# Attention's first query tile in eight units of one batch instead of four of two, and a searched instruction order

## Chip, cores and metric

The kernel runs on one core of one Trainium2 chip. The metric is device microseconds of one execution (lower is better). The median of three executions before the change is 641.2 us (641.05 to 641.68); one further execution was profiled.

## Reference

Sliding-window attention with a linear distance bias, then a mixture of four experts with given probabilities, then one dense block with a squared ReLU:

```python
# q, k, v: [2 batches, 8 heads, 576 positions, 64]; window 128
scores = (q @ k.T) / sqrt(D) - slope[h] * |i - j|     # only 0 <= i - j < 128
attn   = exp(scores - max); attn = attn / (attn.sum(-1) + 1e-9)
x      = attn @ v                                     # reshaped to [1152 tokens, 512]
p      = domain_probs / (domain_probs.sum(-1) + 1e-9)
x      = sum_e p[:, e:e+1] * (relu(x @ w1[e]) @ w2[e])   # 4 experts, 512 -> 1024 -> 512
out    = (relu(x @ w_in) ** 2) @ w_out                # 512 -> 2048 -> 512
```

All inputs and the output are float32.

## The kernel before

**Stages.** Tokens are cut into four chunks (256, 256, 256 and 384 tokens). Attention works in units of query tiles: the first 128 queries of a batch (query tile 0, chunk 0) need only the first 128 keys. Later units cover two query tiles. Expert 0's first three chunks are interleaved with attention, so that TensorE (PE) has expert work to do while VectorE (DVE), ScalarE (ACT) and GpSimd (POOL) prepare the softmax. After that the kernel is a long row of expert matmuls, paced by another mechanism that the change does not touch.

**A unit of query tile 0** ("raw": plain float32, no split into a rounded part and a rest) runs these tasks: `sc` (L863 to L879: scores on PE), `mx` (`top`, L917: bias and running minimum, DVE), `ex` (L926: exp, ACT), `in` (L933, L937: sum and reciprocal, DVE), `no` (L942: normalise, DVE or POOL), `tp` (L966: transpose on PE), `hi` (copy the transposed tile to `pt`, ACT or DVE), `pv` (L764: times v, PE), `evx` (copy the result into the float32 tile `xfirst`), and later `evh` and `evl` (rounded part and rest, `xh` and `xl`). There are four such units; unit `c` holds heads `2c` and `2c+1` of both batches, that is four head squares of 128x128.

**First expert items.** Item `f` of chunk 0 computes 128 of the 1024 hidden columns: `g1.f` (first matmul), `hh` (ReLU), `g2.f` (second matmul into two `y` banks). Items 0 to 3 use `xfirst` and the weights as loaded, in float32, so they wait for no split: `g1` is four matmuls of 256 columns (L1839), one for each 128 rows of `xfirst` (so one for each unit), `g2` is L1790. Weight tiles of 512 KB are loaded in the order w1 part 0 (items 0 and 1), w2 part 0, w1 part 1 (items 2 and 3), w2 part 1, and so on. Items from 4 on use weights split by `weight_parts` (`wh`, `wl`) and run at L1051 and L1287.

**What sets the order.** A list planner (`Plan`) runs while the program is built. Each task has engine options with a modelled time (occupancy and latency), dependencies, buffer slots and a due time. The planner takes the engine that can start earliest, among its tasks that can start within 0.15 us the one due first, and writes that task's instructions at once. Each engine then executes its own instructions in that order. The modelled times count load latency as 4.2 to 4.6 us (5.2 for the second half), and matmuls that start before `COLD` (3.0 us) at 1.7 times their time.

**Fillers.** `keep_busy(place)` (L560) writes small bf16 matmuls on zeros in front of a task on PE, as many as fit into the gap that the planner sees: `int((gap - 0.2) / 0.08)`. (The other branch, `early`, asks for `plan.at["PE"] < 1.0`, but `at` has been advanced past the task by then.) The first scores task has a modelled start of 4.28 us, so 51 fillers stand in front of it.

**First loads.** `first_load(what, half)` issues two DMAs, one per batch: q of both halves and k of half 1 on SP's queue, k of half 0 on ACT's. Then v, then the weight tiles and the loads of later units follow on SP's queue.

Of the kernel before, what the change touches and what calls it, by code (L numbers as in the profile page):

```python
# [16 lines left out]
P = 128  # L17
# [12 lines left out]
class Buf:  # L30
# [3 lines left out]
    def __init__(self, kind):  # L34
        self.kind, self.users, self.end, self.tile = kind, 0, 0.0, None


class Plan:
# [7 lines left out]
    COLD = 3.0  # L46
    WARM = 24.0
    HELD = 0.65
    SLOWED = 0.3

    def __init__(self, slots):
        self.tasks = []
        self.slots = slots
        self.held = {k: [] for k in slots}
        self.at = dict(PE=0.0, ACT=0.0, DVE=0.0, POOL=0.0, SP=0.0)
        self.port = dict(POOL=None, DVE=None)

    def add(
        self, name, opts, fn, deps=(), takes=(), bufs=(), due=0.0, follow=(), cold=True,
        shared=False  # L60
    ):
        t = dict(
            name=name, opts=opts, fn=fn, deps=[d for d in deps if d], takes=list(takes),
            bufs=list(takes) + list(bufs), due=due, end=None, follow=[d for d in follow if d],
            cold=cold, shared=shared,
        )
        for b in t["bufs"]:
            b.users += 1
        self.tasks.append(t)
        return t  # L70

    def ready(self, t):
        r = 0.0
        for d in t["deps"]:
            if d["end"] is None:
                return None
            r = max(r, d["end"] + 0.08)
        for d in t["follow"]:
            if d["end"] is None:
                return None  # L80
            r = max(r, d["start"])
        want = {}
        for b in t["takes"]:
# [3 lines left out]
            if i >= 0:  # L87
                if held[i].users:
                    return None
                r = max(r, held[i].end + 0.08)  # L90
        return r

    def run(self, until=None):
        todo = self.tasks
        while todo and not (until and until()):
            cand = []
            for t in todo:
# [4 lines left out]
                for eng, occ, lat in t["opts"]:  # L102
                    start = max(self.at[eng], r)
# [4 lines left out]
                cand.append((best, t))  # L108
            assert cand, [t["name"] for t in todo[:20]]
            first, _ = min(cand, key=lambda c: c[0][1])  # L110
            eng, start = first[0], first[1]
            (eng, start, occ, lat), t = min(
                (c for c in cand if c[0][0] == eng and c[0][1] <= start + self.LOOK),
                key=lambda c: c[1]["due"],
            )
            other = self.port["POOL" if eng == "DVE" else "DVE"]
            if other and (eng == "POOL" or eng == "DVE" and t["shared"]):
# [3 lines left out]
                else:  # L121
# [4 lines left out]
                    self.at["POOL"] = max(self.at["POOL"], other["start"] + other["occ"])  # L126
                occ, lat = occ + more, lat + more
            t["start"], t["end"], t["occ"] = start, start + lat, occ
            self.gap = start - self.at[eng] if start < self.WARM else 0.0
            self.at[eng] = start + occ  # L130
            if eng == "POOL" or eng == "DVE" and t["shared"]:
                self.port[eng] = t
            for b in t["takes"]:
                self.held[b.kind].append(b)
            t["fn"](eng)
            for b in t["bufs"]:
                b.users -= 1
                b.end = max(b.end, t["end"])
            todo.remove(t)
# [3 lines left out]
def kernel(  # L143
# [346 lines left out]
    def last_runs(nt):  # L490
# [17 lines left out]
        rq=3, rk=2, rv=4, qh=2, ql=2, khl=2, sc=2, tp=2, ts=5, st=5, pt=4, work=2, y=2, h=4  # L508
# [118 lines left out]
    units = [dict(bs=(0, 1), t0=0, t1=1, c=c, col=0) for c in range(NP)]  # L627
# [8 lines left out]
    task = {}  # L636

# [5 lines left out]
    def unit_tasks(u, due):  # L643
        d = units[u]
        bs, t0, t1, c = d["bs"], d["t0"], d["t1"], d["c"]
        nb = len(bs)
        G = 2 * nb
# [5 lines left out]

        raw = t0 == 0
# [59 lines left out]
        if raw:  # L714
            lq, lk, lv = task["first", "q", c // 2], task["first", "k", c // 2], task["first", "v"]
# [31 lines left out]
        if t0 == 0:  # L747
            for i in range(nb):
                mm.append((i, P, 0, 2 * i, i * P, P))
# [7 lines left out]
        def pv(eng):  # L757

            if raw:
                xps = b_["work"].tile = ps_tile("work", [P, nb * nq], "xps")  # L760
                keep_busy(xps[:, 0:P])
                for i in range(nb):
                    for a in range(2):
                        nc.tensor.matmul(  # L764
                            out=xps[a * D:(a + 1) * D, i * P:(i + 1) * P],
                            lhsT=first_in["v"][:, i, (2 * c + a) * D:(2 * c + a + 1) * D],
                            rhs=b_["pt"].tile[:, 2 * i + a, :], start=True, stop=True,
                            skip_group_check=True,
                        )
                if c == NP - 1:  # L770
# [16 lines left out]
        def evx(eng):  # L787
            if not first_x:
                first_x.append(w_tile([P, KT, CHUNKS0[0][1]], F32, "xfirst"))
            rounded(eng, first_x[0][0][:, c, :], b_["work"].tile)  # L790

        def xh_later(eng):
            rounded(eng, xh[:, c, cols], first_x[0][0][:, c, :])

        def xl_later(eng):
            rest(eng, xl[:, c, cols], first_x[0][0][:, c, :], xh[:, c, cols])
# [20 lines left out]
        tpv = add("pv", [pe(0.84 if raw else us)], pv, deps=split + [lv],  # L817
                  takes=[b_["work"]], bufs=used,
                  due=end - 1.3, follow=[prev["pv"]])
        if raw:  # L820
            add("evx", [act(nb * nq), dve(nb * nq)], evx, deps=[tpv], bufs=[b_["work"]],
                due=end - 0.9)
            teh = add("evh", [act(nb * nq), dve(nb * nq)], xh_later, shared=True,
                      deps=[task["evx", u]], due=end + 6.0)
            add("evl", [gps(nb * nq), dve(nb * nq)], xl_later, shared=True, deps=[teh],
                due=end + 7.0)
# [6 lines left out]
    def job_tasks(u, i, t, add, b_, end, ready, G, q0, k0, pos, wide):  # L833
# [22 lines left out]
        def scores(eng):  # L856
# [12 lines left out]
            for g in range(G):  # L869
                if raw:  # L870
                    nc.tensor.matmul(  # L871
                        out=sc[0:n, g, :], lhsT=first_in["q", c // 2][0:D, g // 2, 2 * (c % 2) + g % 2, :],
                        rhs=first_in["k", c // 2][0:D, g // 2, 2 * (c % 2) + g % 2, :],
# [27 lines left out]
        def top(eng):  # L901
# [14 lines left out]
            for g in range(G):  # L916
                nc.vector.tensor_tensor_reduce(  # L917
                    out=s["ts"].tile[0:n, g, :], in0=s["sc"].tile[0:n, g, 0:m],
                    in1=bias[0:n, 2 * c + g % 2, off:off + m], scale=QS, scalar=3.0e38,
# [72 lines left out]
        tb = [task["bias", c, True]] + ([task["bias", c, False]] if t else [])  # L992
# [21 lines left out]
        us_act = squares * 0.22  # L1014
# [641 lines left out]
    def first_load(what, half):  # L1656
        t, buf = w_tile([P, 2, 4, P], F32, "first")
        first_buf.append(buf)
        first_in[what, half] = t
        src = qT if what == "q" else kT  # L1660
        queue = nc.scalar if (what, half) == ("k", 0) else nc.sync
        for b in range(B):
            queue.dma_start(
                out=t[0:D, b], in_=src[b, 4 * half:4 * half + 4, 0:D, 0:P].rearrange("a p s -> p a s")
            )
# [7 lines left out]
    for half in range(2):  # L1673
        for i, what in enumerate("qk"):
            task["first", what, half] = plan.add(
                "first" + what, [("ACT" if (what, half) == ("k", 0) else "SP", 1.3, 5.2 if half else 4.2)],
                lambda eng, what=what, half=half: first_load(what, half), due=half + 0.1 * i,
            )
    task["first", "v"] = plan.add("firstv", [("SP", 2.4, 4.6)], lambda eng: first_v(), due=4.0)
    for u in range(len(units)):  # L1680
        if u < NP:
            unit_tasks(u, [14.0 + 2.0 * u])
        else:
            end = 38.0 + 5.5 * (u - NP)
# [8 lines left out]
    def weight_load(i):  # L1693
# [8 lines left out]
        t = plan.add(f"wl{i}", [("SP", 2.4, 4.6)], load, due=due - 9.0,  # L1702
# [3 lines left out]
    def weight_parts(i):  # L1706
# [27 lines left out]
        j = parted.index(i)  # L1734
        room_ = [task["pv", NP - 1]] if j else []
        if j > 1:
            room_ += [wtask["lo", parted[j - 2], 1], wtask.get(("used", parted[j - 2]))]
        if raw and j > PER - (RAW1 + RAW2) // FTQ + 2:
            room_ += [itask["g2", FT - 1]] + [task["evl", u] for u in range(NP)]
        for h in range(2):  # L1740
            a = wtask["hi", i, h] = plan.add(
                f"wh{i}.{h}", [act(m), dve(m)], lambda eng, h=h: hi(eng, h),
                shared=True, deps=[t] + room_, due=later - 4.0 + h,
                follow=[wtask.get(("hi", i, 0))],
# [3 lines left out]
                shared=True, deps=[a], due=later - 3.0 + h, follow=[wtask.get(("lo", i, 0))],  # L1748
# [10 lines left out]
    wnext["load"] = wnext["ops"] = 0  # L1759

    def first_item(it, f, g1_done, hb, wb, due):
# [17 lines left out]
        a = plan.add(f"hh{it}", [act(n), dve(n)], hf, deps=[g1_done], bufs=[wb], due=due + 1.0)  # L1779
# [4 lines left out]
        def g2(eng):  # L1784
# [15 lines left out]
            takes=ybufs[0] if f == 0 else [], bufs=[] if f == 0 else ybufs[0],  # L1800
            due=due + ITEM * LAG + 2.0, follow=[itask.get(("g2", it - 1))],
        )
        if f % FTQ == FTQ - 1:
            wtask["used", wi] = g
        return lambda: None

    def item_tasks(it):
# [4 lines left out]
        us = [u for u in range(len(units)) if u // NP == ch]  # L1812
        wi = 2 * (f // FTQ)

        split = it < 4
        raw = ch == 0 and f < RAW1
# [5 lines left out]
        def mm(eng, ks):  # L1822
            if not split:
                hb["ps"] = ps_tile("work", [P, n], "hps")
            else:
                if ks[0] == 0 and half == 0:
                    wb.tile = ps_tile("y", [P, 2, n], "hps")
                hb["ps"] = wb.tile[:, half, :]
            if ch:
                gemm1_mm(hb["ps"], 0, ch, f, ks, 0)  # L1830
                return
            if KT - 1 in ks:
                x_done()
            if f >= RAW1:
                gemm1_mm(hb["ps"], 0, ch, f, ks, half if split else 0)
                return
            cs = slice((f % FTQ) * P, (f % FTQ + 1) * P)
            for k in ks:
# [191 lines left out]
```

## Time and profile before

| | before |
|---|---|
| median of 3 executions | 641.2 us (641.05 to 641.68) |
| profiled execution | 641.43 us, span of the core 639.7 us |
| PE busy | 633.3 us (99%) |
| DVE, ACT, POOL busy | 470.3, 299.3, 384.3 us |
| instructions | 11060 |
| DMA | 64.70 MB, mean 101 GB/s |

Busy time of PE includes the fillers, which compute nothing. The profiled execution is 1.73 us longer than its span, which is what lies around it.

### The profile page before, as it was taken

Reading aid. Unit: us, or ns where it says so; the run is one execution under the profiler, and the core shown is the slowest. Engines: PE = TensorE matmul, PEld = TensorE weight load, DVE = VectorE, ACT = ScalarE, POOL = GpSimd, SP = SyncE. Lnnn points to the kernel's source line nnn. Section 1 sums busy time; section 2 is a strip of 40 time slices with the busy share of each in tenths; the row PEclk is TensorE's granted clock in tenths of the full one; section 3 lists DMA queues with packets and bytes.
Section 4 is the critical chain, followed back from the end, with each engine's and each line's share of the span. In section 5 each row is a group of like instructions: output and inputs, shape, how many; then the busy total and the mean of one; then the engine's idle time right before and its main releaser. Section 6 shows DMA issues by size and latency. Waiting matters only on the chain.

```text
span 639.7 us, 11060 instructions
## 1 busy us (share of the span) xinstructions
PE 633.3 (99%) x3929; PEld 569.2 (89%) x3929; DVE 470.3 (74%) x1023; ACT 299.3 (47%) x763; POOL 384.3 (60%) x497
## 2 busy tenths in 40 slices
PE   9999999999999999999999999999999999999997
PEld 8778899899898898998998998999999898998996
DVE  6999975378897877777777777768768767667463
ACT  6998765135354344344334334345554544343230
POOL 2589776179667447447447446346687786766531
PEclk9999999999999999999999999999999999999999
DMA  9964330222133444434434434312123223001012
GB/s 233 265 159 104 98 94 26 99 66 99 34 116 115 133 132 127 134 119 141 129 112 157 130 107 127 119 69 67 34 77 124 82 83 116 17 1 51 1 66 83
DMA packets 46983, 64.70 MB, mean 101 GB/s; under 512 B 6480, under 2 KB 29264, under 8 KB 46928
## 3 DMA queue, kind: packets, MB, share of 16 engines
q1 hardware_dynamic: 35520, 39.48, 20.9%
q10 hardware_dynamic: 11408, 24.51, 12.9%
q8 instruction: 31, 0.51, 0.3%
q14 instruction: 24, 0.20, 0.1%
HBM read 53.23 MB, written 10.75 MB: 100 GB/s over the span
## 4 chain that ended last, share of the span: by engine, by line
PE 98%; ACT 1%; DVE 0%; POOL 0%; issue 0%; POOLq 0%
PE yacc L1261 38%; PE hps L1170 35%; PE hps L1051 7%; PE yacc L1287 7%; PE xps L778 2%; PE sc L879 2%; PE tp L966 1%; PE hps L1839 1%; PE yacc L1790 1%; PE sc L560 1%; PE xtp L1353 1%; PE sc L863 1%; ACT ts L926 1%; PE sc L871 0%; PE xps L764 0%; PE ylast L1261 0%
## 5 line engine op out<-in xcount | busy, mean ns | idle before, releaser
L1261 PE MATMUL yacc<-wh,hmem 128*128 128x512 f32 x716 | 228.0, 390 | 0.0
L1261 PEld LDWEIGHTS yacc<-wh,hmem 128*128 128x128 f32 x716 | 134.6, 188 | 27.0
L1261 PE MATMUL yacc<-wl,hmem 128*128 128x512 f32 x358 | 139.9, 391 | 0.0
L536 POOL TENSOR_TENSOR wl<-wraw,wh 128x256 fp32r<-128x256 f32 (+1 forms) x79 | 74.0, 962 | 39.3 <-ACT wh L469 27.7
L536 POOL TENSOR_TENSOR hmem<-c,hmem 128x320 fp32r<-128x320 f32 (+1 forms) x64 | 59.3, 944 | 60.4 <-ACT hmem L1201 60.4
L536 POOL TENSOR_TENSOR ls<-wsum,hs 128x256 fp32r<-128x256 f32 x77 | 61.4, 825 | 54.3 <-ACT hs L414 53.6
L1185 DVE TENSOR_TENSOR u<-hps,p 128x256 f32<-128x256 f32 (+1 forms) x80 | 36.4, 455 | 65.0 <-PE hps L1170 63.1
L1181 ACT ACTIVATE p<-hps 128x256 f32<-128x256 f32 (+1 forms) x80 | 32.8, 410 | 108.8 <-PE hps L1170 108.7
L1261 PEld LDWEIGHTS yacc<-wl,hmem 128*128 128x128 f32 x358 | 67.3, 188 | 12.4
L307 DVE SCALAR_TENSOR_TENSOR wconv<-wraw,wconv 128x512 int32<-128x512 int32 x64 | 58.1, 907 | 1.3
L536 POOL TENSOR_TENSOR la<-wraw,ha 128x256 fp32r<-128x256 f32 x54 | 48.6, 919 | 16.7 <-ACT ha L400 16.7
L1205 ACT ACTIVATE hmem<-c 128x256 fp32r<-128x256 f32 (+1 forms) x72 | 31.3, 445 | 52.8 <-DVE c L1185 51.1
L1206 DVE SCALAR_TENSOR_TENSOR hmem<-c,hmem 128x256 fp32r<-128x256 f32 (+1 forms) x72 | 42.7, 614 | 14.0 <-ACT hmem L1205 13.0
L1201 ACT ACTIVATE hmem<-c 128x320 fp32r<-128x320 f32 (+1 forms) x64 | 27.3, 445 | 52.4 <-DVE c L1195 33.6
L1170 PE MATMUL hps<-ht,ls 128*128 128x320 f32 (+1 forms) x160 | 47.5, 297 | 1.3 <-POOL ls L536 1.3
L1170 PE MATMUL hps<-xh,hs 128*128 128x320 f32 (+1 forms) x160 | 47.7, 298 | 0.0
L1170 PE MATMUL hps<-ht,hs 128*128 128x320 f32 (+1 forms) x160 | 47.6, 297 | 0.0
L1170 PE MATMUL hps<-lt,hs 128*128 128x320 f32 (+1 forms) x160 | 47.4, 296 | 0.0
L1170 PE MATMUL hps<-xl,hs 128*128 128x320 f32 (+1 forms) x160 | 47.4, 296 | 0.0
L1170 PE MATMUL hps<-xh,la 128*128 128x320 f32 (+1 forms) x160 | 47.4, 296 | 0.0
L1170 PE MATMUL hps<-xl,ha 128*128 128x320 f32 (+1 forms) x160 | 47.4, 296 | 0.0
L1170 PE MATMUL hps<-xh,ls 128*128 128x320 f32 (+1 forms) x160 | 47.4, 296 | 0.0
(164 smaller groups left out, 1640.1 us busy)
## 6 DMA issues: line engine op xcount, KB each, us to landing
wraw<-in_w_dram SPq DMA_DIRECT2D x32, 512.0 KB, 3.9
wraw<-in_w_out_dram ACTq DMA_DIRECT2D x16, 512.0 KB, 3.9
w<-wconv ACTq DMA_DIRECT2D x32, 256.0 KB, 4.1
wraw<-w SPq DMA_DIRECT2D x16, 512.0 KB, 3.7
wraw<-in_w_in_dram ACTq DMA_DIRECT2D x14, 512.0 KB, 4.2
rq<-in_qT_dram SPq DMA_DIRECT2D x8, 256.0 KB, 7.7
out_dram<-y SPq DMA_DIRECT2D x7, 256.0 KB, 2.1
rk<-in_kT_dram SPq DMA_DIRECT2D x8, 192.0 KB, 5.6
```

The source lines that it names most:

```text
L307: nc.vector.scalar_tensor_tensor(out=ai, in0=raw[j][:, :, part], scalar=amount, in1=ai, op0=op, op1=ALU.bitwise_or,)
L536: e.tensor_tensor(out=out, in0=in0, in1=f32(in1), op=ALU.subtract)
L778: nc.tensor.matmul(out=xps[a * D:(a + 1) * D, x, o0:o0 + w], lhsT=held["rv"].tile[0:r, k, a * D:(a + 1) * D], rhs=held["pt"].tile[0:r, a, ...
L1051: nc.tensor.matmul(out=ps, lhsT=l_[:, k, cs], rhs=r_[:, k, cols], start=(k == 0 and r_ is xh and l_ is wh and not second), stop=(k == KT - ...
L1170: nc.tensor.matmul(out=ps, lhsT=a[l_][:, k, :], rhs=b[r_][:, k, :], start=start and k == 0 and l_ == r_, stop=stop and k == 1 and l_ == 1, ...
L1181: nc.scalar.activation(out=out, in_=x, func=ACTF.Copy)
L1185: nc.vector.tensor_tensor(out=out, in0=x, in1=y, op=ALU.add)
L1201: nc.scalar.activation(out=hh, in_=r, func=ACTF.Copy)
L1205: nc.scalar.activation(out=hh, in_=src, func=ACTF.Relu)
L1206: nc.vector.scalar_tensor_tensor(out=hl, in0=src, scalar=0.0, in1=f32(hh), op0=ALU.max, op1=ALU.subtract)
L1261: nc.tensor.matmul(out=y, lhsT=l_[:, ns], rhs=r_[:, fo, cols], start=(first and fo == 0 and j == 0), stop=(last and fo == FTQ - 1 and j == 2),
L1287: nc.tensor.matmul(out=y, lhsT=l_[:, ns], rhs=r_[:, fo, :], start=(first and j == 0), stop=(last and j == 2),)
```

## The change

Query tile 0 is cut into eight units, `(batch, c)` with two heads each. `first_load` is one DMA for one batch, and the batch 0 halves are issued first. `pv`, `sc` and `mx` handle two head squares; `evx` writes 128 columns of `xfirst`; `evh` and `evl` run once for two units. `g1` of items 0 to 3 becomes eight matmuls of 128 columns (batch, then 128-row part) in place of four of 256. The leading fillers are counted as `int((gap - 0.9) / 0.107)` when the gap is over 3 us, and `COLD` is 6.2. The planner no longer writes instructions while it plans: it lays the whole plan, then tries 600 variations of the due times near PE's modelled waits, keeps one if the modelled end of PE is not later, and writes the best order. The weight buffers (18 places, `wb`) are modelled as slots in the plan, instead of hand-written dependencies (`room_`). Some modelled times differ. The cut diff:

```diff
-    COLD = 3.0
+    COLD = 6.2
+    ROUNDS = 600
+    FREE = ("wb",)
...
+    def run(self):
+        chance = random.Random(1)
+        due = [t["due"] for t in self.tasks]
+        least, order, waits = self.lay(due)
...
+        for _ in range(self.ROUNDS):
+            if not waits:
+                break
+            to, _ = chance.choices(waits, [w for _, w in waits])[0]
+            trial = list(due)
+            for i, s in enumerate(starts):
+                if to - 10.0 < s < to + 3.0 and chance.random() < 0.15:
+                    trial[i] += chance.gauss(0.0, 4.0)
+            end, o, w = self.lay(trial)
+            if end is not None and end <= least:
+                least, order, waits, due = end, o, w, trial
+                starts = [t["start"] for t in self.tasks]
...
     def keep_busy(place):
-        early = plan.at["PE"] < 1.0 and plan.gap > 2.0
-        lead, each = (0.6, 0.11) if early else (-0.2, 0.08)
+        lead, each = (-0.9, 0.107) if plan.gap > 3.0 else (-0.2, 0.08)
         for _ in range(int(max(plan.gap + lead, 0.0) / each)):
...
-    units = [dict(bs=(0, 1), t0=0, t1=1, c=c, col=0) for c in range(NP)]
+    NR = B * NP
+    units = [dict(bs=(b,), t0=0, t1=1, c=c, col=b * P) for b in range(B) for c in range(NP)]
...
-                xps = b_["work"].tile = ps_tile("work", [P, nb * nq], "xps")
+                xps = b_["work"].tile = ps_tile("work", [P, nq], "xps")
...
-            rounded(eng, first_x[0][0][:, c, :], b_["work"].tile)
+            rounded(eng, first_x[0][0][:, c, cols], b_["work"].tile)
...
-    for half in range(2):
-        for i, what in enumerate("qk"):
-            task["first", what, half] = plan.add(
-                "first" + what, [("ACT" if (what, half) == ("k", 0) else "SP", 1.3, 5.2 if half else 4.2)],
-                lambda eng, what=what, half=half: first_load(what, half), due=half + 0.1 * i,
-            )
-    task["first", "v"] = plan.add("firstv", [("SP", 2.4, 4.6)], lambda eng: first_v(), due=4.0)
+    for b in range(B):
+        for half in range(2):
+            for i, what in enumerate("qk"):
+                n = 2 * b + half
+                if (what, half) == ("k", 0):
+                    opts = [("ACT", 0.7, 5.2 if b else 3.9)]
+                else:
+                    opts = [("SP", (1.2, 0.6, 0.6, 0.6)[n], 4.6)]
+                task["first", what, half, b] = plan.add(
+                    "first" + what, opts,
+                    lambda eng, what=what, half=half, b=b: first_load(what, half, b),
+                    due=b + 0.1 * half + 0.01 * i, takes=[] if b else [q_places[2 * half + i]],
+                    follow=[task["first", what, half, 0]] if b else [],
+                )
+    task["first", "v"] = plan.add("firstv", [("SP", 2.4, 5.8)], lambda eng: first_v(), due=4.0,
+                                  takes=[q_places[4]])
...
+        def mm_raw(eng, b, k):
...
+            cs, at = slice((f % FTQ) * P, (f % FTQ + 1) * P), slice(b * P, (b + 1) * P)
+            nc.tensor.matmul(
+                out=hb["ps"][:, at], lhsT=wtask["raw", wi][:, k, cs],
+                rhs=first_x[0][0][:, k, at], start=begin, stop=(k == KT - 1),
+                skip_group_check=True,
+            )
```

## Rows read from the trace of the kernel before

**Rows 1.** Page, part 2: granted TensorE clock in 40 slices, tenths of full speed.

```profile
PEclk9999999999999999999999999999999999999999
```

**Rows 2.** Busy time by stretch: PE, PEld (weight loads), DVE, ACT, POOL, clock, DMA.

```profile
10.00:15.00 5.00, 4.73 (x53) 4.21 (x54) 4.69 (x26) 4.81 (x25) 0.00 (x0) 1.00 1.08 318
...
40.00:50.00 10.00, 10.00 (x61) 8.01 (x60) 9.25 (x35) 9.82 (x35) 9.02 (x12) 1.00 0.66 185
50.00:60.00 10.00, 10.00 (x81) 8.75 (x81) 9.35 (x31) 9.33 (x28) 9.79 (x15) 1.00 0.29 78
...
80.00:100.00 20.00, 20.00 (x169) 18.17 (x169) 13.25 (x60) 12.46 (x44) 13.83 (x31) 1.00 0.32 85
```

**Rows 3.** Timeline of PE, 1 to 20 us: start, duration, what, count.

```profile
1.06 5.62 PE L560 MATMUL sc<-idle 128*128 128x128 bf16 x51 [1.06 <-DVE idle L1635]
6.61 2.08 PE L871 MATMUL sc<-first 64*128 64x128 f32 x16
8.82 1.11 PE L560 MATMUL sc<-idle 128*128 128x128 bf16 x17
...
17.28 0.60 PE L1839 MATMUL hps<-xfirst,wraw 128*128 128x256 f32 x2
```

**Rows 4.** Chain of work that ended last, 0 to 130 us: start, duration, what.

```profile
11.38 3.20 ACT ts L926 x16
...
15.64 0.63 PE tp L966 x4
...
17.88 1.02 PE xps L764 x16
18.90 1.49 PE hps L1839 x6
...
23.38 0.43 PE hps L1839 x2
...
42.90 0.22 PE tp L966 x2
```

**Rows 5.** DMA issues in order of issue: KB, us from issue to landing.

```profile
first<-in_qT_dram SPq DMA_DIRECT2D x1, 128.0 KB, 3.8
first<-in_kT_dram ACTq DMA_DIRECT2D x1, 128.0 KB, 3.1
...
first<-in_qT_dram SPq DMA_DIRECT2D x1, 128.0 KB, 4.7
...
first<-in_v_dram SPq DMA_DIRECT2D x1, 512.0 KB, 5.6
...
wraw<-in_w_dram SPq DMA_DIRECT2D x1, 512.0 KB, 6.7
...
wraw<-in_w_dram SPq DMA_DIRECT2D x2, 512.0 KB, 9.5
```

**Rows 6.** Timeline of SP's queue: issue start, issue time, what, count.

```profile
0.80 3.02 SPq L1663 DMA_DIRECT2D first<-in_qT_dram  x4
...
5.19 0.60 SPq L1671 DMA_DIRECT2D first<-in_v_dram  x1
5.83 0.47 SPq L227 DMA_DIRECT2D wraw<-in_w_dram  x1
...
7.55 1.24 SPq L227 DMA_DIRECT2D wraw<-in_w_dram  x2
```

**Rows 7.** Groups of DVE and ACT, 5 to 20 us: busy us, mean ns | idle before.

```profile
L917 DVE CUSTOM_DVE_ANT_0 ts<-sc,bias 128x128 f32<-128x128 f32 x16 | 3.7, 287 | 4.0 <-PE sc L871 3.8
L942 DVE TENSOR_TENSOR ts<-ts,st 128x512 f32<-128x512 f32 x4 | 2.8, 691 | 0.1
...
L937 DVE RECIPROCAL st<-st 128x4 f32<-128x4 f32 x4 | 0.7, 178 | 0.1
...
L933 DVE TENSOR_REDUCE st<-st 128x4 f32<-128x8 f32 x4 | 0.6, 154 | 0.1
...
L926 ACT ACTIVATE ts<-ts,st 128x128 f32<-128x128 f32 x16 | 6.2, 389 | 3.4 <-DVE st L917 3.3
```

More of the change, by code (lines that the diff above doesn't have):

```diff
@@ L34, in __init__ @@
     def __init__(self, kind):
-        self.kind, self.users, self.end, self.tile = kind, 0, 0.0, None
+        self.kind, self.users, self.left, self.end, self.tile = kind, 0, 0, 0.0, None
 class Plan:
@@ L53, in __init__ @@
         self.slots = slots
-        self.held = {k: [] for k in slots}
-        self.at = dict(PE=0.0, ACT=0.0, DVE=0.0, POOL=0.0, SP=0.0)
-        self.port = dict(POOL=None, DVE=None)
+        self.gap = 0.0
     def add(
@@ L63, in add @@
             name=name, opts=opts, fn=fn, deps=[d for d in deps if d], takes=list(takes),
-            bufs=list(takes) + list(bufs), due=due, end=None, follow=[d for d in follow if d],
-            cold=cold, shared=shared,
+            bufs=list(takes) + list(bufs), due=due, follow=[d for d in follow if d],
+            cold=cold, shared=shared, next=[],
         )
@@ L68, in add @@
             b.users += 1
+        for d in t["deps"] + t["follow"]:
+            d["next"].append(t)
         self.tasks.append(t)
@@ L86, in ready @@
             i = len(held) + n - 1 - self.slots[b.kind]
-            if i >= 0:
-                if held[i].users:
+            if i < 0:
+                continue
+            if b.kind in self.FREE:
+                ends = sorted(x.end for x in held if not x.left)
+                if i >= len(ends):
+                    return None
+                r = max(r, ends[i] + 0.08)
+            else:
+                if held[i].left:
                     return None
@@ L91, in ready, with lay @@
         return r
[L93 to L97, printed above, removed]
+    def lay(self, due):
+        self.held = {k: [] for k in self.slots}
+        at = dict(PE=0.0, ACT=0.0, DVE=0.0, POOL=0.0, SP=0.0)
+        port = dict(POOL=None, DVE=None)
+        cand, order, waits = [], [], []
+        for i, t in enumerate(self.tasks):
+            t["due_now"], t["open"] = due[i], len(t["deps"]) + len(t["follow"])
+            for b in t["bufs"]:
+                b.left, b.end = b.users, 0.0
+            if not t["open"]:
+                cand.append(t)
+        while cand:
+            ways, first = [], None
+            for t in cand:
                 r = self.ready(t)
@@ L107, in run @@
                         best = (eng, start, occ, lat)
[L108 to L111, printed above, removed]
+                ways.append((best, t))
+                if first is None or best[1] < first[1]:
+                    first = best
+            if first is None:
+                return None, order, waits
             (eng, start, occ, lat), t = min(
-                (c for c in cand if c[0][0] == eng and c[0][1] <= start + self.LOOK),
-                key=lambda c: c[1]["due"],
+                (w for w in ways if w[0][0] == first[0] and w[0][1] <= first[1] + self.LOOK),
+                key=lambda w: w[1]["due_now"],
             )
-            other = self.port["POOL" if eng == "DVE" else "DVE"]
+            other = port["POOL" if eng == "DVE" else "DVE"]
             if other and (eng == "POOL" or eng == "DVE" and t["shared"]):
@@ L125, in run @@
                     other["end"] += self.HELD * both
-                    self.at["POOL"] = max(self.at["POOL"], other["start"] + other["occ"])
+                    at["POOL"] = max(at["POOL"], other["start"] + other["occ"])
                 occ, lat = occ + more, lat + more
             t["start"], t["end"], t["occ"] = start, start + lat, occ
-            self.gap = start - self.at[eng] if start < self.WARM else 0.0
-            self.at[eng] = start + occ
+            gap = start - at[eng]
+            if eng == "PE" and gap > 0.05 and len(order) and start > self.COLD:
+                waits.append((start, gap))
@@ L131, in run @@
+            order.append((t, eng, gap if start < self.WARM else 0.0))
+            at[eng] = start + occ
             if eng == "POOL" or eng == "DVE" and t["shared"]:
-                self.port[eng] = t
+                port[eng] = t
             for b in t["takes"]:
                 self.held[b.kind].append(b)
+            for b in t["bufs"]:
+                b.left -= 1
+                b.end = max(b.end, t["end"])
+            cand.remove(t)
+            for d in t["next"]:
+                d["open"] -= 1
+                if not d["open"]:
+                    cand.append(d)
@@ new lines, in lay @@
+        return (at["PE"] if len(order) == len(self.tasks) else None), order, waits
+    def run(self):
+        chance = random.Random(1)
+        due = [t["due"] for t in self.tasks]
+        least, order, waits = self.lay(due)
+        assert least is not None, [t["name"] for t in self.tasks if t["open"]][:20]
+        starts = [t["start"] for t in self.tasks]
[10 more added lines that the diff above has]
+                least, order, waits, due = end, o, w, trial
+                starts = [t["start"] for t in self.tasks]
+        self.least = least
+        for t, eng, gap in order:
+            self.gap = gap if eng == "PE" else 0.0
@@ L636 @@
     task = {}
+    x_place, q_places = Buf("wb"), [Buf("wb") for _ in range(5)]
+    raw_place = {i: Buf("wb") for i in range(2 * NQ)}
+    h_place = {}
     def x_done():
@@ L714, in unit_tasks @@
         if raw:
-            lq, lk, lv = task["first", "q", c // 2], task["first", "k", c // 2], task["first", "v"]
+            lq, lk = (task["first", x, c // 2, bs[0]] for x in "qk")
+            lv = task["first", "v"]
         else:
@@ L820, in unit_tasks @@
         if raw:
[L821 to L826, printed above, removed]
+            add("evx", [act(nq), dve(nq)], evx, deps=[tpv],
+                takes=[x_place] if u == 0 else [], bufs=[b_["work"]], due=end - 0.9,
+                follow=[task.get(("evx", 0))])
+            if c % 2 == 0:
+                return
+            teh = add("evh", [act(2 * nq), dve(2 * nq)], xh_later, shared=True,
+                      deps=[task["evx", u - 1], task["evx", u]], due=end + 6.0)
+            add("evl", [gps(2 * nq), dve(2 * nq)], xl_later, shared=True, deps=[teh],
+                bufs=[x_place], due=end + 7.0)
+            for x in ("evh", "evl"):
+                task[x, u - 1] = task[x, u]
             return
@@ L990, in part @@
             )
-        tb = [task["bias", c, True]] + ([task["bias", c, False]] if t else [])
+        tb = [task["bias", c, own] for own in (True, False)[0:1 + (t > 0)]]
         if twin:
@@ L1654, with first_load @@
     first_in, first_buf, first_x, first_h = {}, [], [], {}
[L1656 to L1659, printed above, removed]
+    def first_load(what, half, b):
+        if b == 0:
+            first_in[what, half], buf = w_tile([P, 2, 4, P], F32, "first")
+            first_buf.append(buf)
         src = qT if what == "q" else kT
         queue = nc.scalar if (what, half) == ("k", 0) else nc.sync
[L1662 to L1665, printed above, removed]
+        queue.dma_start(
+            out=first_in[what, half][0:D, b],
+            in_=src[b, 4 * half:4 * half + 4, 0:D, 0:P].rearrange("a p s -> p a s"),
+        )
     def first_v():
@@ L1700, in load @@
             wtask["raw", i] = raws[i][0][0].rearrange("p (k f) -> p k f", k=nk)
-        t = plan.add(f"wl{i}", [("SP", 2.4, 4.6)], load, due=due - 9.0,
+        t = plan.add(f"wl{i}", [("SP", 2.4, 4.6)], load, due=due - 9.0, takes=[raw_place[i]],
                      follow=[wtask.get(("load", i - 1))])
@@ L1732, in weight_parts @@
         m = n * nf
[L1734 to L1739, printed above, removed]
+        places = [Buf("wb"), Buf("wb")]
+        for x in places:
+            x.users += 1
         for h in range(2):
@@ L1742, in weight_parts @@
                 f"wh{i}.{h}", [act(m), dve(m)], lambda eng, h=h: hi(eng, h),
-                shared=True, deps=[t] + room_, due=later - 4.0 + h,
-                follow=[wtask.get(("hi", i, 0))],
+                shared=True, deps=[t, task["pv", NR - 1]], due=later - 4.0 + h,
+                takes=[] if h else places, follow=[wtask.get(("hi", i, 0))],
             )
@@ L1777, in hf @@
                 )
-        a = plan.add(f"hh{it}", [act(n), dve(n)], hf, deps=[g1_done], bufs=[wb], due=due + 1.0)
+        if f % 4 == 0:
+            h_place[f // 4] = Buf("wb")
+        place = h_place[f // 4]
+        a = plan.add(
+            f"hh{it}", [act(n), dve(n)], hf, deps=[g1_done], takes=[] if f % 4 else [place],
+            bufs=[wb], due=due + 1.0, follow=[h_first[0]] if f % 4 else [],
+        )
+        if f % 4 == 0:
+            h_first[:] = [a]
         wi = 2 * (f // FTQ) + 1
```

140 lines of the change are left out of this document (63 added, 77 removed).

## Prediction, made before the change was run

> **What bounds the kernel now.** I read the page's busy shares first, then busy time by stretch, then the chain of waits, then PE's timeline and the landing of the loads in the first 20 us.
>
> PE is busy through the whole span, and from 40 to 100 us it is busy without a break [rows 2]. So the end of the kernel is PE's useful work plus whatever PE does not use. That loss lies almost wholly at the start. There "busy" deceives: 51 fillers stand from 1.06 to 6.6 us, and more follow at 8.82 [rows 3]. Count the useful work up to 15.64, from where the chain stays on PE [rows 4]: the scores of 16 head squares, 32 records at 2.08/16 = 0.13 us [rows 3], 4.16; two transposed units of the four, 8 records at 0.11 [rows 4], 0.88; one pv, 8 records at 1.02/16 = 0.064, 0.5. That is 5.5 of 15.64, so 10.1 is lost. The three following tasks up to 17.4 lose some 0.3 more (0.63 instead of 0.44 at 15.64): **10.4 us of start loss**. A change of the start can win at most this.
>
> After 17.4 us the loss is small. Against each task's fastest pace the chain loses 0.9 us from 17 to 31 us (for example 1.49 us for six records that take 0.43 a pair elsewhere, 0.2 lost [rows 4]), and summed the same way some 2.9 us up to 121 us. This is all that a better order could win there.
>
> What holds the start? The first scores come at 6.61 [rows 3]. DVE idles 3.8 us for them and ACT 3.3 [rows 7]; then ACT's 16 exponentials are the chain, the last of them in the row from 11.38 to 14.58 [rows 4]. At 10 to 15 us DVE and ACT are over 90% busy, POOL does nothing, and the DMA share is 1.08 [rows 2]. From 40 to 60 us DVE, ACT and POOL are each over 90% busy, so helpers have little room there; from 80 us on they do [rows 2].
>
> **The change part by part.**
>
> *First scores.* They need all four loads of the half. The second q, issued near 1.6, lands 4.7 later, at 6.3 [rows 5, 6]; fillers, 5.6 us for a modelled 4.1, end just behind. After: one q (0.80 + 3.8 = 4.6) and one k on ACT's queue (3.1 to land) suffice [rows 5, 6]. The modelled start is 4.6 + 0.08 = 4.68, so the count is int(3.78/0.107) = 35 fillers; at the 5.62/51 = 0.11 us that they take now [rows 3] they end at 1.06 + 3.85 = 4.9. Scores start at 4.9: 1.7 us earlier, most of it from the loads, since with the old loads shorter fillers alone would have won only 6.6 - 6.3 = 0.3.
>
> *First softmax.* `mx` waits for a whole unit of scores, now 4 records (0.5 us) instead of 8 (1.0). So DVE starts at about 5.5 and ACT at 5.8, about 2.3 us earlier. The exponentials are as many as before, 16 at 0.4. Those of two units end at 7.4. The next need the third load of SP's queue, which I put at 7.0 (a slot of 0.8 behind the second, with its latency); a gap of 0.5 follows. The other twelve take 4.8, and some 0.4 of copies will lie between: they end near 13.1 instead of 14.6. The gain on this chain shrinks to 1.5.
>
> The granted clock reads full speed, 2.4 GHz, in every slice [rows 1], yet the first 51 fillers take 0.11 us each and the 17 at 8.82 only 0.065 [rows 3]. If the earlier scores ran at 1.2 GHz, four records would take at most double: 0.5 us more on the first unit, and since a gap of 0.5 lies behind units 0 and 1 it would mostly be absorbed there. I take nothing; the bound, 0.5, is rival D. *The Trainium skill, "TensorE: Matmul & The Clock Gate", Part 1, says that the array starts throttled and that activity releases it, so fewer leading fillers would put the first scores onto the slow clock. The fillers' 0.11 us agree with it, the granted-clock row does not show it.*
>
> *When PE is full.* Two loads set the floor. v lands at 5.19 + 5.6 = 10.8, so no pv starts before; the first weight tile lands at 5.83 + 6.7 = 12.5 [rows 5, 6]. The loads ahead of them are the same number and size, only reordered, so I keep these times. By 12.6 units 0 to 3 have passed pv (from 10.85: four at 0.26, each followed by a copy of about 0.3), so g1 of items 0 and 1 for batch 0 can start, where now the first g1 starts at 17.28 [rows 3]. Useful by then: all scores 4.16, five transposed units 1.1, four pv 1.04, together 6.3. Loss: 12.6 - 6.3 = 6.3.
>
> *From 12.6 on.* The weight tile of items 2 and 3 is the second of the pair issued from 7.55; the pair's median to landing is 9.5 and the tile lands near 18.5. Until then PE has g1 of items 0 and 1 for both batches (16 matmuls at 0.26, 4.2), three transposed units (0.7) and four pv (1.0): 5.9 us for 5.9 us. It just covers, if batch 1's softmax keeps up; scores of the next units fill what is left. Every interruption costs about 0.2 [rows 4]. I add 0.5 for batch 1 being late and 0.5 for three interruptions: **loss after 7.3, bounds 6.3 and 9.0. Gain 10.4 - 7.3 = 3.1.**
>
> *g1 in two halves.* 16 matmuls of 256 columns take 0.43 each [rows 4], 6.9 us. The 32 of 128 columns have double the weight loads. If only columns counted, they would also take 6.9 (bound: nothing). The nearest row is the scores, also 128 float32 columns with 128 weight columns: 0.26 each [rows 3], 32 x 0.26 = 8.3, **1.4 us more of PE's time**, not hidden, since PE is full. I take 1.4 because that row has the same size. It has 64 rows of weights, not 128.
>
> *Helpers.* Four more sums and reciprocals, 4 x (0.154 + 0.178) = 1.3 us of DVE [rows 7]. Normalising, copying `pt` and `evx` are cut in half too; between nothing more and double. From 0.69 us for 512 columns [rows 7], a third of it fixed, I estimate some 2 us over all. DVE, ACT and POOL share 3.3 us, 1.1 each; they start 2.3 us earlier and POOL's empty 10 to 15 us [rows 2] can take normalising. I take nothing, and up to 1.5 lost between 40 and 80 us where no helper has room.
>
> *Search and buffer model.* They can only win from the 2.9 us behind 17.4; part of it (0.2 at each interruption) is no wait of the plan. Bounds: 1.5 won, 1.5 lost, since a modelled order packed to the last tenth leaves no margin for real lateness. I take nothing. The order of later stages is untouched.
>
> **Sum:** -3.1 + 1.4 = -1.7 us. Profiled execution 641.43 becomes 639.7; the median 641.2 becomes **639.5**.
>
> **Rivals.**
>
> *A. More is won.* The 128-column g1 costs little (for it: nothing but the columns bound), and the search finds 1 us or more. Loss 6.5, g1 +0.5, order -1: -3.9 - 1 + 0.5 = -4.4, **636.8**. Against it: the scores row.
>
> *B. Nothing is left.* The loads and helpers hold PE: the loss is 8.5 (batch 1 late, since ACT and DVE are already over 90% busy), helpers cost 0.5 later. -1.9 + 1.4 + 0.5 = 0, **641.2**. For it: DMA share 1.08 and the helpers' shares [rows 2].
>
> *C. Slower: PE stands at a weight tile in its own order.* The model lands a weight tile 4.6 us after issue; the rows say 6.7 and 9.5 [rows 5]. Today this is harmless because PE reaches g1 only at 17.3. After the change PE reaches it at 12.6, in an order fixed by the model. If items 2 and 3 stand ahead of batch 1's part of items 0 and 1, PE waits from 14.7 to 18.5, 3.8 us, with pv and transposes queued behind it, and softmax behind them. -3.1 + 3.8 + 1.4 = +2.1, **643.3**. It decides once the start loss is over 9.0 (10.4 - 1.4). Against it: transposes and scores are there to be put between.
>
> *D. A slow first unit.* The first scores run at half speed and the gap behind them does not absorb it: -1.7 + 0.5 = -1.2, **640.0**. For it: the fillers' 0.11 us. Against it: the granted clock [rows 1], and today's scores at 6.61, right behind those fillers, take 0.13 us a record, too little for half speed: a g1 record of 256 columns takes 0.215 [rows 4], so one of 128 would take 0.11 at full and 0.215 at half speed.
>
> **How the numbers follow.** As forecast (638.3 to 640.6) 0.42; A 0.20; B 0.18; C 0.12; D 0.08. A measurement tells apart about 0.2%, 1.3 us: faster means under 639.9, slower over 642.5. Of the forecast's own 0.42, some 0.34 lies under 639.9; with A, and a little of B and D, faster gets 0.58. Slower gets C and a little of B, 0.14; the rest, 0.28, is the same. Range: 636.6 (A) to 642.4 (between B and C); what lies outside is half of A's better part and most of C, some 2 in 10.
>
> **What would show it.** Scores near 4.9 and DVE's first `mx` near 5.5; about 35 fillers in front; the first g1 near 12.6 instead of 17.3; 32 g1 matmuls at 0.26 in a full stretch; fillers and waits before 18 us summing to 7.3. The prediction is wrong if g1 starts after 15 us, if a wait for a weight tile shows on PE before 20 us, if a g1 matmul costs 0.22, or if new PE waits of over 1 us together show between 30 and 100 us.

## The result, and the profile after

The kernel became slower: 647.99 us median (647.36 to 648.16, four executions) against 641.35 (four executions too), ratio 1.01 with a 95% interval of 1.0087 to 1.0114. The prediction was 639.5 us with a range of 636.6 to 642.4: wrong in sign, outside its range and above its slowest rival (C, 643.3). The profiled execution took 647.97 us, span 646.2.

First the page (span, busy time and granted clock in slices, as in [rows 1]), then busy time by stretch with the columns of [rows 2]:

```profile
span 646.2 us, 11046 instructions
PE 639.1 (99%) x3907; PEld 572.8 (89%) x3907; DVE 469.3 (73%) x1036; ACT 298.7 (46%) x763; POOL 386.2 (60%) x507
PEclk9999999999999999999999999999999999999999
```

```profile
10.00:15.00 5.00, 5.00 (x21) 3.69 (x23) 1.91 (x13) 2.52 (x10) 0.92 (x3) 1.00 1.08 319
15.00:20.00 5.00, 5.00 (x29) 3.89 (x26) 2.70 (x16) 2.60 (x12) 2.33 (x2) 1.00 1.14 277
...
40.00:50.00 10.00, 10.00 (x74) 7.69 (x73) 9.36 (x27) 10.00 (x31) 9.80 (x14) 1.00 0.47 139
```

PE is as busy as before, but from 10 to 15 us it executes 21 matmuls in place of 53, and DVE and ACT are 38% and 50% busy where they were over 90% [rows 2]. So PE is the slow one, without a wait. Its timeline shows why; the like lines of the kernel before stand in [rows 3, 4]:

```profile
1.06 3.91 PE L607 MATMUL sc<-idle 128*128 128x128 bf16 x35 [1.06 <-DVE idle L1694]
4.90 3.17 PE L930 MATMUL sc<-first 64*128 64x128 f32 x12
...
9.91 1.22 PE L930 MATMUL sc<-first 64*128 64x128 f32 x4
11.07 0.69 PE L1025 MATMUL tp<-ident,ts 128*128 128x128 f32 x2
...
16.66 0.63 PE L1908 MATMUL hps<-xfirst,wraw 128*128 128x128 f32 x2
...
18.38 1.12 PE L814 MATMUL xps<-pt,first 128*64 128x128 f32 x8
...
21.33 0.70 PE L814 MATMUL xps<-pt,first 128*64 128x128 f32 x4
21.96 0.69 PE L1025 MATMUL tp<-ident,ts 128*128 128x128 f32 x2
22.44 1.51 PE L1908 MATMUL hps<-xfirst,wraw 128*128 128x128 f32 x8
23.88 0.44 PE L814 MATMUL xps<-pt,first 128*64 128x128 f32 x4
24.25 0.44 PE L1025 MATMUL tp<-ident,ts 128*128 128x128 f32 x2
```

The scores do start at 4.90, with 35 fillers in front. But a record (one matmul of the trace) of scores takes 3.17/12 = 0.26 to 1.22/4 = 0.30 us where it took 0.13 [rows 3], and one of pv 1.12/8 = 0.14 where it took 0.064 [rows 4]. This lasts until about 23.4 us, in the midst of the eight records that start at 22.44; behind them four records of pv take 0.44 us, where those at 21.33 still took 0.70, and two of a transpose 0.44 in place of 0.69. PE ran at half pace for its first 23 us. The granted clock reads 1.00 throughout: this trace holds no clock record ahead of its first change, at 23.4 us, and the view prints full speed there. Below, "the clock is up" means 2.4 GHz and "down" 1.2 GHz: by the trace's records where it has them, by the pace of like records where it has none. Of executions without a kept trace only the time and the mean granted clock are on record.

To locate the loss I summed every PE task at its fastest pace and subtracted that from the time, as the prediction did for its "start loss":

```
us lost by            10     15     20     25     35     60     120
before               7.8    9.4   10.5   10.8   11.3   12.1   14.5
after                7.8   10.7   13.4   15.5   17.0   18.7   20.7
```

Against the kernel before, 5.7 us more are lost by 35 us, another 0.9 by 60 us (0.7 of it is one wait of PE for a tile that POOL normalises; it shows again in experiment 13), nothing more later. The sums in the experiments are made the same way.

Executions of one kernel differ by when the clock rises and whether it falls again in the first 25 us, so for kernels near that edge single executions are given beside the median.

### The profile page after: what moved, and what is told of

The parts are those of the page before. It is cut to its first block, busy times and chain, and to the rows that moved or that the text cites. A ratio compares the mean times of both kernels' runs of the same rounds, so it can differ in the third digit from the quotient of the medians.

```text
span 646.2 us, 11046 instructions
## 1 busy us (share of the span) xinstructions
PE 639.1 (99%) x3907; PEld 572.8 (89%) x3907; DVE 469.3 (73%) x1036; ACT 298.7 (46%) x763; POOL 386.2 (60%) x507
## 4 chain that ended last, share of the span: by engine, by line
PE 96%; POOL 2%; ACT 1%; DVE 0%; issue 0%; POOLq 0%
PE yacc L1320 38%; PE hps L1229 35%; PE yacc L1346 7%; PE hps L1110 6%; PE xps L827 2%; PE tp L1025 2%; PE sc L938 1%; PE hps L1908 1%; PE sc L930 1%; PE sc L607 1%; PE xtp L1412 1%; PE xps L814 1%; POOL ts L1014 1%; PE sc L922 1%; POOL wl L584 0%; POOL pt L1046 0%
## 5 line engine op out<-in xcount | busy, mean ns | idle before, releaser
L584 POOL TENSOR_TENSOR wl<-wraw,wh 128x256 fp32r<-128x256 f32 (+1 forms) x81 | 77.5, 982 | 39.2 <-ACT wh L517 27.7
L1320 PEld LDWEIGHTS yacc<-wl,hmem 128*128 128x128 f32 x358 | 67.3, 188 | 12.5
L584 POOL TENSOR_TENSOR la<-wraw,ha 128x256 fp32r<-128x256 f32 x54 | 48.6, 920 | 16.7 <-ACT ha L448 16.7
L1260 ACT ACTIVATE hmem<-c 128x320 fp32r<-128x320 f32 (+1 forms) x64 | 27.3, 446 | 52.3 <-DVE c L1254 33.5
```

Of the source, the lines that this page charges most:

```text
L584: e.tensor_tensor(out=out, in0=in0, in1=f32(in1), op=ALU.subtract)
L1260: nc.scalar.activation(out=hh, in_=r, func=ACTF.Copy)
L1320: nc.tensor.matmul(out=y, lhsT=l_[:, ns], rhs=r_[:, fo, cols], start=(first and fo == 0 and j == 0), stop=(last and fo == FTQ - 1 and j == 2),
```

## Experiments

Theory 1: fewer leading fillers keep TensorE at half pace. Theory 2: not the clock but the new order, searched against a model, is late on the chip. All times are us; each group of experiments has its own runs of the kernel before (medians 641.3 to 641.6).

**1. The kernel before with 35 leading fillers.**

```diff
-        lead, each = (0.6, 0.11) if early else (-0.2, 0.08)
+        lead, each = (-0.9, 0.0955) if plan.gap > 3.0 else (-0.2, 0.08)
```

> The kernel before, with 35 leading fillers in place of 51 and nothing else. Theory 1 (TensorE stays at half pace because fewer fillers stand in front): the raw scores take near 0.29 us a record in place of 0.13 and the first full-pace task comes after 15 us; 644 to 648 us. Theory 2 (the new order, not the clock, costs the time): 0.13 us a record and 641 us, within 0.5.

Measured: 645.18 median. Eight of ten executions took 645.1 to 647.1, two 641.05 and 641.15, which is the time of the kernel before. Busy time by stretch of the profiled one (645.42), then two rows of PE's timeline:

```profile
4.20:7.50 3.30, 2.06 (x19) 1.75 (x17) 0.37 (x3) 0.67 (x5) 1.66 (x5) 0.96 1.20 191
7.70:17.70 10.00, 10.00 (x67) 9.10 (x68) 6.40 (x38) 6.28 (x32) 0.00 (x0) 0.51 1.08 308
17.90:30.00 12.10, 12.10 (x90) 9.75 (x87) 9.48 (x31) 11.04 (x31) 5.00 (x6) 1.00 0.73 198
```

```profile
8.48 2.00 PE L560 MATMUL sc<-idle 128*128 128x128 bf16 x17
10.40 3.78 PE L871 MATMUL sc<-first 64*128 64x128 f32 x16
```

Here the trace has the records: the clock rose to 2.4 GHz at 3.8 us, fell to 1.2 GHz at 7.2 after fillers to 4.5, four score records, two waits for loads (0.45 and 0.79 us) and part of the next scores, and came back at 17.5, though PE was busy all the while from the fall on. Between, the fillers at 8.48 took 2.00 us for 17, against 1.11 [rows 3], and the scores at 10.40 took 0.24 us a record, against 0.13. The fillers alone, with nothing else of the change, cost 3.7 us: theory 1 for this part, by the two executions too. In detail it misses: some ten score records came before the fall, and those behind it took 0.24 us, not 0.29.

**2. The changed kernel with the old filler formula (55 leading fillers).** `lead, each = (-0.2, 0.08)`.

> The changed kernel with the old count of leading fillers, some 55 in place of 35, and nothing else. Theory 1: full pace from about 7 us, raw scores at 0.13 us a record, first g1 before 16 us; 636 to 641 us. Theory 2: still 646 to 648 us.

Measured: 646.87 median, in two groups: 642.28, 643.27 and 643.30 with a mean granted clock of 0.999, and 645.73 to 648.49 with 0.988 to 0.992. So 55 fillers raise the clock (at 5.9 us in the profiled execution) but do not always hold it; with it up the same order is 5 us faster. Yet 642.3 to 643.3 is still over 641.4, and none of the eight lies in theory 1's 636 to 641.

**3. The changed kernel without the search**, `ROUNDS = 0`, 35 fillers.

> The changed kernel without the search (600 rounds become 0), 35 fillers. Theory 1: still half pace until after 20 us; 646 to 650 us. Theory 2 (the searched order stalls on the chip): back to 641 to 643 us.

Measured: 645.17 (643.59 to 645.36): better than the changed kernel, slower than before. Busy time by stretch of the profiled one (643.59):

```profile
6.30:9.50 3.20, 3.04 (x22) 2.15 (x20) 2.86 (x25) 3.04 (x16) 1.61 (x6) 0.97 1.09 265
9.70:16.40 6.70, 6.70 (x31) 5.35 (x31) 2.80 (x19) 4.10 (x17) 2.46 (x8) 0.52 1.10 335
16.60:30.00 13.40, 12.93 (x113) 11.32 (x113) 11.21 (x44) 11.42 (x41) 8.26 (x11) 1.00 0.86 232
```

The clock rose at 5.9 us, in the midst of the scores, fell at 9.3 after a stretch in which PE ran scores nearly without a pause (busy 3.04 of 3.20 us), with five fillers between, and was back at 16.2. No long wait of PE is needed for a fall. Both theories miss: theory 2 expected 641 to 643, theory 1 expected 646 to 650 and half pace until after 20 us. Why the clock was back earlier than in the changed kernel, no run here shows.

**4. Both: 55 leading fillers, no search.**

> The changed kernel with some 55 leading fillers and without the search. Theory 1: full pace from about 7 us; what is left against the same with the search is the search's worth, which I put at 0 to 3 us; 638 to 643 us. Theory 2: 641 to 643 us, as without the search and with 35 fillers.

Measured: 641.68, ratio to before 1.0009 (0.9987 to 1.0031). Nine executions 640.8 to 642.0, one 648.40 with a granted clock of 0.988: 6.7 us between clock up and down in one and the same kernel. With the clock up and no search, the smaller units neither win nor lose.

**5 to 8. Holding the clock with early fillers.** `keep_busy` gets a least count: 5 ahead of every raw score, the first four raw transposes and the first two raw pv.

```diff
-    def keep_busy(place):
+    def keep_busy(place, least=0):
...
-        for _ in range(int(max(plan.gap + lead, 0.0) / each)):
+        for _ in range(max(least, int(max(plan.gap + lead, 0.0) / each))):
...
-            keep_busy(sc[:, 0, 0:P])
+            keep_busy(sc[:, 0, 0:P], 5 if raw else 0)
```

> The changed kernel with its 35 leading fillers, and at least 5 fillers ahead of each of the eight raw scores, the first four raw transposes and the first two raw pv. Theory 1 (clock): first scores stay at 4.9 us and may run at half pace, but the clock rises before 9 us and stays up in nearly every execution; against the changed kernel's 648, 639 to 643 us, spread of the executions under 2 us. Theory 2 (the searched order alone is late): 646 us or more.

> The same with early fillers, and without the search. If the search's order costs 1 to 2 us on its own, as the full-pace executions of the two kernels with 55 fillers suggest (642.3 to 643.3 with, 640.8 to 642.0 without), this is 1 to 2 us below the kernel with early fillers and search; with scores at 4.9 in place of 6.5 us, 639 to 641 us. If the search is worth something, it is above it.

> The same with early fillers, with the search started from another random seed. If the search's loss is that of one unlucky order, this lies elsewhere by over 1 us, perhaps below the unsearched one; if it is a loss of any order packed by the model, it lies within 1 us of the first seed and above the unsearched one.

> Early fillers, no search, and 55 leading fillers in place of 35: the first scores at 6.5 us in place of 4.9. If the start of the scores sets the end, 1 to 1.6 us above the kernel with 35; if helpers take it back later, within 0.5 us of it.

Measured: with search 644.29 (643.64 to 644.48, no execution near 648), without 644.31, another seed 643.56, with 55 leading fillers and no search 645.65. The clock holds (but for one execution at 649.03 in eight without the search and one at 648.44 in ten with the other seed), 3.7 us come back; the rest I put down to the fillers' own price. By the sum, 2.8 us are lost from 10 to 15 us, against 1.1 in experiment 4: each score now follows the last by 1.03 us, five fillers (0.38) and four records (0.64). Search or not makes no difference under them, so these four do not tell its worth, and my 639 to 641 without it misses. With 55 leading fillers the time is 1.3 us above that with 35 (645.65 against 644.31): under five fillers a task, the start of the scores does reach the end.

**9 to 12. Fewer early fillers.** At least 2 ahead of seven raw scores, two transposes and two pv (`a_few`); 3, 3 and 0 (`a_sc3`); 2 with 45 leading fillers, `lead = 0.2` (`a_f45_few`).

> The changed kernel, 35 leading fillers, at least 2 (in place of 5) ahead of seven raw scores, the first two raw transposes and the first two raw pv. If 2 hold the clock up, the fillers' own price falls by some 2 us against the kernel with 5: 641 to 643 us. If they do not, executions at 646 to 648 us come back.

> The same without the search. With the clock up 640 to 642 us; below the one with search if the search costs 1 to 1.6 us, above it if the search is worth something; executions with the clock down 644 to 648 us.

> No search, 35 leading fillers, at least 3 ahead of seven raw scores and the first two raw transposes, none ahead of pv. Clock up: 641 to 643 us, between 2 and 5 fillers; fewer slow executions than with 2.

> No search, 45 leading fillers (first scores near 5.9 us), at least 2 ahead of the same tasks. Clock up more often than with 35; if the start of the scores sets the end, 1 us above the kernel with 35 in executions at full pace: 641 to 643 us.

Measured: with 2 and the search 648.16, all four executions at 647.8 or more; without the search 648.06, four executions at 641.48 to 641.98 and six at 648.0 to 649.3; with 3, 644.29, five at 641.4 to 642.6 and five at 646.0 to 649.0; with 45 leading fillers and 2, **641.91, all ten at 641.6 to 642.7**, ratio 1.0009 (1.0000 to 1.0019).

Two things follow. PE at 1.2 GHz has the pace of the changed kernel. This is `a_few`, where the trace has the clock, in busy time by stretch and in PE's timeline; compare 1.22, 0.69 and 1.12 us above:

```profile
9.50:23.00 13.50, 13.50 (x69) 9.90 (x69) 4.75 (x29) 6.39 (x24) 4.17 (x6) 0.51 1.11 310
```

```profile
18.12 1.22 PE L930 MATMUL sc<-first 64*128 64x128 f32 x4
19.27 1.12 PE L814 MATMUL xps<-pt,first 128*64 128x128 f32 x8
20.32 0.69 PE L1025 MATMUL tp<-ident,ts 128*128 128x128 f32 x2
```

And with the clock up and at most two early fillers a task, the start of the scores does not set the end: 4.9 us (`a_few`, no search), 5.0 (45 leading fillers, clock up at 3.9 in the profiled execution) and 6.5 (55) all give 640.8 to 642.7. Time lost by 15 us: 8.8, 8.6 and 8.6; by 35 us: 11.4, 11.2 and 11.2, against 11.3 before. My expectation of 1 us for the later start misses.

**13 and 14. The search with the clock up**: 45 leading fillers and 2, `ROUNDS = 600`, two seeds.

> The kernel with 45 leading fillers and at least 2 ahead of the early raw tasks, now with the search (600 rounds, first seed). Without the search it stands at 641.9 us with all ten executions at full pace. If the searched order is late in itself, 643 to 644 us with all executions close together; if the search only looked bad because the clock fell in some executions, within 0.5 us of 641.9.

> The same with another seed. If every order packed by the model loses on the chip, 642.5 to 644 us; if the first seed was unlucky, 640.5 to 642 us.

Measured: first seed 642.96 (nine at 642.2 to 643.7, one 648.67), second 641.99 (nine at 641.9 to 642.8, one 649.03), unsearched 641.91. The first seed's order, the change's own, costs 1.0 us (0.8 with each group's runs of the kernel before subtracted); the second nothing that shows. Neither wins. The two fences are the waits of PE from 10 to 60 us (us, times, longest), first of the searched order (first seed), then of the unsearched one:

```profile
PE tp L1025 <- POOL ts L1014: 0.7, 1, 0.7
PE tp L1025 <- DVE st L992: 0.6, 1, 0.6
PE hps L1908 <- ACT hfirst L1841: 0.5, 1, 0.5
```

```profile
PE hps L1908 <- ACT hfirst L1841: 0.5, 1, 0.5
```

In the first, two transposes stand at the head of PE's queue before their softmax is normalised, 1.3 us together.

**15. The old count in another place**: the kernel before, 35 fillers ahead of the first and 16 ahead of the second scores (`keep_busy(..., 16 if u == 1 else 0)`).

> The kernel before with 35 fillers in front of the first scores and the other 16 ahead of the second scores: the old count, 51, in another place. If the number of early fillers holds the clock, all executions at full pace and, with the second scores about 1 us later, 641 to 642.5 us; if the unbroken leading row does, executions near 645 us come back, as with 35 alone.

Measured: 642.24; seven executions 641.8 to 642.5, three 647.8 to 648.5 (the profiled one, 648.50, had the clock down until 20.3 us). Against 35 alone the executions at full pace are many more, but not all: neither of my two readings holds fully. The unbroken row of 51 has shown no execution over 643.03 among all those of the kernel before in these experiments.

## Why the prediction was wrong

**The step that failed is rival D's price.** The text said of a half-speed start: "four records would take at most double: 0.5 us more on the first unit", absorbed in a gap. The fillers' 0.11 us were read rightly as the sign of 1.2 GHz, and then the price was taken for one unit, as if the clock would rise by itself right after. It rose at 23.4 us, so every task up to there ran at half pace. With the searched order and the clock up (experiment 13, 642.96, and the full-pace executions of 2) the kernel is some 5 us faster than with it down; experiment 1 shows 3.7 us for the fillers alone, experiments 4 and 9 to 12 show 6 to 7 us between executions of one kernel. The 16 fillers were counted as waste of 0.3 us; their worth was the clock. A row that I had spoke for it: the first 51 at 0.11 us, the scores behind them at 0.13 [rows 3], so the rise came about the end of that very row (the first clock record of that trace is at 6.7 us). Against rival D the text held that today's scores run at 0.13; but they stood behind 51 fillers, and the change takes away 16. *The Trainium skill, "TensorE: Matmul & The Clock Gate", Part 1, says that activity releases the throttle; the runs agree only in part: the clock rose at 5.9 us under a row of 55 fillers (experiment 2), but in the changed kernel PE was busy from 1.06 us on and it rose at 23.4.*

**The search was taken as nothing; it cost 0.1 to 1.0 us** (experiments 12 to 14), inside the bound of 1.5. It also undid a premise: the text kept the landing of the first weight tile, 12.5 us, since the loads ahead of it were the same. The searched order puts a load of k for later units in front. These are SP's queue in the changed kernel, the time to landing of its first weight tile, and PE in experiment 2 with the clock up:

```profile
5.82 0.60 SPq L723 DMA_DIRECT2D rk<-in_kT_dram  x1
6.47 0.59 SPq L275 DMA_DIRECT2D wraw<-in_w_dram  x1
```

```profile
wraw<-in_w_dram SPq DMA_DIRECT2D x1, 512.0 KB, 7.4
```

```profile
14.00 0.46 PE L1908 MATMUL hps<-xfirst,wraw 128*128 128x128 f32 x2 [0.26 <-DMA wraw<-in_w_dram]
```

So the tile lands at 6.47 + 7.4 = 13.9, and at full pace PE stands 0.26 us for it. The 6.6 us then divide into 647.99 - 642.96 = 5.0 for the clock (with somewhat other fillers), 642.96 - 641.91 = 1.05 for the searched order and 641.91 - 641.33 = 0.6 for the rest, which was not taken apart (eight units, fillers, loads for one batch each, buffer model, modelled times).

**The gain of 3.1 us at the start did not come, also with the clock up.** Its parts, in experiments 4 and 12 where nothing else is said: scores at 4.9 came true in the changed kernel (5.0 in experiment 12); first g1 was forecast at 12.6 and came near 13.4 (17.3 before), or at 16.7 in the changed kernel at half pace. But "loss after 7.3" is 9.5 by 20 us, against 10.5 before, and the last 1.0 is gone by 35 us. Half of that 1.0 is one wait of PE for `hfirst`, which ACT makes (0.47 us at 27.3 in experiment 12): every profiled kernel with eight units has it, the kernel before has not. "Three interruptions, 0.5" is the term that was too small. The chain of the kernel with 45 leading fillers shows the price of small tasks:

```profile
11.14 0.64 PE sc L930 x4
11.78 0.22 PE xps L607 x2
11.99 0.37 PE xps L814 x4
...
13.54 0.45 PE hps L1908 x4
```

Four score records take 0.64 us, 0.16 each and not 0.13; four of pv 0.37, 0.093 and not 0.064. Eight units of that are 8 x 0.64 - 4.16 = 1.0 us of scores and up to 8 x 0.37 - 2.05 = 0.9 us of pv more than four large ones: nearly the rest of the gain. What holds the start between 10 and 15 us once scores come early was not tried by itself: in that stretch PE's chain is unbroken, so I put it on these tasks and the fillers between them, but this is argued, not shown.

**g1 in halves was too dear in my sum**: a record takes 0.45/4 = 0.11 us, near the columns bound, not 0.13. Of the 1.4 us some 0.3 is left (summed over the two chains, all of these g1 take 8.07 us in experiment 12 and 7.63 before).

**Rivals.** A: no kernel here beats the one before. B's end (nothing left) is what the change gives without its fillers and search. C did not show: no PE wait for a weight tile of over 0.3 us in any profiled execution up to 35 us.

## What to carry to other kernels

Work that only fills a gap may hold a clock: before you cut it, look at the pace of like records right ahead of it and behind it, and price the loss as half pace for all that follows until something raises the clock, not for the next task. Judge a kernel near such an edge by its single executions, since a median of two groups hides both. Splitting a chain into smaller units starts it earlier, but each small task pays on the engine that was full already; and an order packed to a model's last tenth needs a comparison on the chip against the unsearched one.

## What the runs showed of the hardware

- The granted clock in the view is full speed ahead of the first recorded change, whatever the pace: 1.00 from 0 to 23.4 us in the changed kernel, with score records at 0.26 to 0.30 us.
- The clock can fall with PE hardly idle: at 9.3 us in experiment 3, with PE busy 3.04 of 3.20 us from 6.3 to 9.5. It then stayed at 1.2 GHz for 6.8 to 13.7 us in the profiled executions (experiments 1, 3 and 9), with PE busy almost throughout. In the changed kernel PE was busy from 1.06 us on, and the pace was that of 1.2 GHz until 23.4.
- The same kernel can take 641.5 or 648.1 us (experiment 10). The profiled execution, 641.98, had the clock up from 5.7 us; those at 648 left no trace. That their clock was down is read from experiment 9, the same fillers with the searched order: 648.40, and down from 9.1 to 22.8 us.
